# Windowed attention and a softplus feed-forward on one core: downs two slots later, GpSimd's attention work moved, weights converted between the first heads

## The chip, the cores and the metric

The kernel runs on one core of a Trainium2 chip. The metric is device time in microseconds (us). The engines are TensorE (PE, matmuls, with its weight loads shown apart as PEld), VectorE (DVE), ScalarE (ACT), GpSimd (POOL) and SyncE (SP, which here only issues DMAs).

## The reference

Inputs are q, k, v of 8 batches, 8 heads, 576 positions and 64 values per head, and two weights, 512 x 2048 and 2048 x 512, drawn at random; q, k and v are float32, the weights float64.

```python
scores = (q @ k.T) / sqrt(64)               # per batch and head
mask   = 0 <= i - j < 64                    # a causal window of 64 positions
attn   = softmax(where(mask, scores, -1e9)) # the sum gets + 1e-9
x      = (attn @ v) as 4608 tokens x 512
h      = x @ w_in                           # 4608 x 2048
g      = maximum(h, 0) + log1p(exp(-abs(h)))
out    = g @ w_out                          # 4608 x 512
```

## The kernel before

**Tiling.** Tokens are cut into 12 blocks g of 384 (`TB`), the 8 heads into 4 head pairs hp, the 2048 inner features into 16 chunks f of 128. For float32 precision nearly every matrix is split into a high and a low part (`x0/x1`, `g0/g1`, `w..0/w..1`), and a product is three matmuls: high-high, high-low, low-high.

**Feed-forward.** A step (g, f) is an *up* (`ffn_up`, 12 matmuls of L391 into one of two `ps_h` buffers; then abs, exp, ln on ACT in L395 to L397, the softplus sum L399 on DVE, which is the last reader of `ps_h`, the cast L401 to the high part and the subtraction L402 to the low part) and a *down* (`ffn_down`, 9 matmuls of L412 into the three accumulators `ps_o`). After the last chunk of a block L430 copies `ps_o` to a tile `raw`, and DMAs write it out. The order of steps is `passes`: block 0 with its first 8 chunks (its partial sums go to DRAM and are added again later, L428), block 1 with all 16, block 0 with the other 8, then blocks 2 to 11, 192 steps in all.

**Weights.** `load_w(f)` fetches chunk f as 64-bit words (1 MB, each float64 seen as two 32-bit words), makes float32 of them with one ACT and four DVE instructions (L165 to L169), and splits them: cast on ACT (L172), subtraction on POOL (L173). Even and odd chunks go through two sets of buffers (`raw`/`osb`, `raws`/`ws`).

**Attention.** `attention(g, hp)` is a generator in stages: loads, splitting of q and k (L238 to L243), scores of three sub-blocks (L258 with the masked minimum L265), softmax (L271 to L281) with the splitting of the probabilities (L300 to L308, a transpose by DMA) and of v (L316 to L320), and two stages of attn @ v, one per head (L367, L372, L373), the second of which splits the result to `x_t` by the helper `split` (L150, L151). Blocks 0 and 1 (`by_pe`) take another way: block-diagonal k tiles (`kbd`), transposes on PE (L288), padded v tiles (`v_pad`), in plain float32.

**The order of the work.** Every stage and step gets a place in slots, two slots per step: an up of step n at 2n + 0.5, its down at 2n + 3.5, weights of chunk f at 12 slots (`AHEAD`) before the step that first uses them, an attention stage at the base of its block and head pair plus an offset of its stage (`BASE`, `PACE`, `STG0`, `STG2` for blocks 0 to 2; 8 slots per head pair, `SHP`, for the others). The program is emitted in the order of these places. A planner then orders each engine's queue by priority and by its own costs; from slot 100 on (`PE_ORDERED_FROM`, step 50) PE's queue alone keeps the written order. Tiles of one name (or tag) share `bufs` buffers, and a new one waits until the old one's last reader is done.

Of the kernel before, what the change touches and what calls it, by code (L numbers as in the profile page):

```python
# [15 lines left out]
P = 128  # L16
# [5 lines left out]
NCH = TB // CH + 1  # L22

SPLIT = 8
AHEAD = 12
BASE = (-100, -46, 2 * (SPLIT + 16) - 24)
PACE = (5, 5, 5)
STG0 = (-6, -6, 1, 2, 3, 4, 7, 8)
STG2 = (-10, -5, 0, 1, 2, 3, 14, 15)
STG = (-14, -8, 0, 1, 2, 3, 15, 17)  # L30
SH, SHP = -13, 8
PE_ORDERED_FROM = 100
# [6 lines left out]
def window_attention_softplus_ffn(  # L39
# [70 lines left out]
    for t in range(2):  # L110
        nc.gpsimd.memset(kbd[D:P, t, 0, :], 0.0)
        nc.gpsimd.memset(kbd[0:D, t, 1, :], 0.0)
        nc.gpsimd.memset(kbd[0:D, t, 0, 0:CH], 0.0)
        nc.gpsimd.memset(kbd[D:P, t, 1, 0:CH], 0.0)

# [15 lines left out]
    ident = cpool.tile([P, P], F32, name="ident")  # L131
# [6 lines left out]
    pt_s = spare(1, [P, 2, 2, TB], F32, "pt")  # L138


    v_pads = []
    for n in range(NP):
        t = spare(2 + n, [P, 2, NJ, 2, P], F32, f"v_pad{n}")
        (nc.gpsimd if n else nc.vector).memset(t, 0.0)
        v_pads.append(t)

    mm, tp = nc.tensor.matmul, nc.tensor.transpose

    def split(dst_hi, dst_lo, src, e_hi, e_lo):
        e_hi.tensor_copy(dst_hi, src)  # L150
        e_lo.tensor_tensor(dst_lo, src, dst_hi.bitcast(F32), ALU.subtract)  # L151

    def load_w(f):


        if f % 2 and f < NE + 4:
            raw, w = spare(6, [P, 2, DM], w_words.dtype, "raws"), spare(7, [P, 2, DM], F32, "ws")
        else:
            raw = ff.tile([P, 2, DM], w_words.dtype, name="raw", bufs=1)
            w = ff.tile([P, 2, DM], F32, name="osb", bufs=1)  # L160
        nc.sync.dma_start(raw, w_words[f])
        words = raw.bitcast(U32).rearrange("p m (n two) -> p two m n", two=2)
        low, high = words[:, 0, :, :], words[:, 1, :, :]
        wb = w.bitcast(U32)
        nc.scalar.activation(w, high.bitcast(F32), AF.Abs)  # L165
        nc.vector.tensor_scalar(w, w, ZERO_HIGH, None, ALU.max)
        nc.vector.tensor_scalar(wb, wb, 3, 0x3FFFFFF8, ALU.logical_shift_left, ALU.bitwise_and)
        nc.vector.scalar_tensor_tensor(wb, high, 0xC0000000, wb, ALU.bitwise_and, ALU.bitwise_or)
        nc.vector.scalar_tensor_tensor(wb, low, 29, wb, ALU.logical_shift_right, ALU.bitwise_or)  # L169
        for m in range(2):  # L170
            hi, lo = [weight(m, i, f) for i in range(2)]
            nc.scalar.copy(hi, w[:, m, :])  # L172
# [6 lines left out]
    def attention(g, hp):  # L179
# [15 lines left out]
        if by_pe:  # L195
            qf = ld.tile([P, 2, TB], F32, name="q_in") if hp % 2 else ld.tile([P, 2, W - P + TB], F32, name="k_in")
            qf = qf[:, 0, 0:TB]
            kf = kbd[:, hp % 2, :, :]
# [4 lines left out]
            v_pad = v_pads[hp]  # L203

            def load_v(rows, lay, j0, start):
                n = rows.stop - rows.start
                for j in range(j0, NJ):
                    dst = v_pad[rows, lay, j, :, :].rearrange("p h (i d) -> p (h i) d", i=2)[:, 0:4:3, :]
                    s = start + j * P
                    nc.sync.dma_start(dst, v[s : s + n, c0 : c0 + P].rearrange("p (h d) -> p h d", h=2))  # L210

            if t0 == 0:
                dst = v_pad[CH:P, 0, 0, :, :].rearrange("p h (i d) -> p (h i) d", i=2)[:, 0:4:3, :]
                nc.sync.dma_start(dst, v[0:CH, c0 : c0 + P].rearrange("p (h d) -> p h d", h=2))
            load_v(slice(0, P), 0, 1 if t0 == 0 else 0, t0 - CH)
            load_v(slice(0, CH), 1, 0, t0 + CH)
            load_v(slice(CH, P), 1, 0, t0)
        else:
            q_in = ld.tile([P, 2, TB], F32, name="q_in")
            k_in = ld.tile([P, 2, W - P + TB], F32, name="k_in")  # L220
            v_in = ld.tile([P, NCH, P], F32, name="v_in")
            ts, ks = slice(t0, t0 + TB), slice(t0 - CH, t0 + TB)
            for half in heads:
                nc.sync.dma_start(
                    q_in[half, :, :], qT[c0 : c0 + P, ts].rearrange("(h d) t -> d h t", h=2)
                )
                nc.sync.dma_start(
                    k_in[half, :, :], kT[c0 : c0 + P, ks].rearrange("(h d) t -> d h t", h=2)
                )
            for half in heads:  # L230
                nc.sync.dma_start(v_in[half, :, :], v[ks, c0 : c0 + P].rearrange("(c p) n -> p c n", p=CH))
        yield

        if not by_pe:
# [8 lines left out]
            nc.vector.tensor_tensor(k_lo, k_in, k_hi.bitcast(F32), ALU.subtract)  # L243
# [37 lines left out]
        nc.vector.tensor_tensor(pn, pn, sm.unsqueeze(2).to_broadcast([P, 2 * NJ, P]), ALU.mult)  # L281
        if by_pe:

            pt = pt_s[:, hp % 2, :, :]
            for hh in range(2):
                pp = bank()
                for j in range(NJ):
# [2 lines left out]
        else:  # L290
# [15 lines left out]
            nc.gpsimd.tensor_tensor(part(1, 0), pv[0], part(0, 1), ALU.subtract)  # L306
# [9 lines left out]
            nc.scalar.copy(v12[:, :, :, 0, :], vv)  # L316
            nc.vector.tensor_tensor(vv, vv, v12[:, :, :, 0, :], ALU.subtract)  # L317
            nc.scalar.copy(v12[:, :, :, 1, :], vv)  # L318
            nc.gpsimd.tensor_tensor(v13[low, :, :, :], vv[low, :, :, :], v12[low, :, :, 1, :], ALU.subtract)  # L319
            nc.vector.tensor_copy(v13[up, :, :, :], v12[up, :, :, 0, :])  # L320
        yield

# [11 lines left out]
        for hh in range(2):  # L334
# [48 lines left out]
    def ffn_up(g, f):  # L383
# [13 lines left out]
        nc.scalar.activation(u, u, AF.Ln, bias=1.0)  # L397
        gf = u
        nc.vector.scalar_tensor_tensor(gf, hv, 0.0, u, ALU.max, ALU.add)  # L399
        gt = [ff.tile([P, TB], F32R, name=f"g{i}", bufs=2) for i in range(2)]  # L400
        (nc.scalar.copy if g == 0 else nc.vector.tensor_copy)(gt[0], gf)  # L401
        (nc.vector if g >= 2 else nc.gpsimd).tensor_tensor(gt[1], gf, gt[0].bitcast(F32), ALU.subtract)  # L402
        gs[g, f] = gt

    def ffn_down(g, f, first, last):
# [10 lines left out]
        if last:  # L416
            rows = out[ORDER[g] * TB : (ORDER[g] + 1) * TB, :]
            spill, fill = f < NF - 1, f == NF - 1 and g in part
            if spill:
                part[g] = rows = dram.tile([TB, DM], F32, name="part")  # L420
            o = ff.tile([P, 2, DM], w_words.dtype, name="raw", bufs=1).bitcast(F32).rearrange("p a n -> p (a n)").rearrange("p (j n) -> p j n", n=DM)
            for j0, j1 in ((0, 2), (2, 3)):
                rs = slice(j0 * P, j1 * P)
                if fill:
                    nc.sync.dma_start(o[:, j0:j1, :], part[g][rs, :].rearrange("(j p) n -> p j n", p=P))
                for j in range(j0, j1):
                    if fill:
# [82 lines left out]
```

## Time and profile before

| what | value |
|---|---|
| median of 3 runs | 1280.91 us (1280.70 to 1281.58) |
| the profiled execution | 1280.53 us, span 1278.7 us |
| granted TensorE clock, mean | 0.912 |
| PE busy | 1092.9 us (85%), 5888 matmuls |
| DVE busy | 849.5 us (66%) |
| ACT busy | 690.9 us (54%) |
| POOL busy | 295.5 us (23%) |

A line of the profile names engine, line of the kernel, operation, tiles written <- read, shapes, count, busy time and the mean of one in ns, then the idle time of the engine before these instructions and what ended it. "PE ps_o L412 <- DVE g L401" reads: PE's matmuls of line 412 stood idle until DVE's instruction of line 401 was done. In the chart of the span in 40 equal slices a digit is the share of a slice in tenths:

```profile
PE   6668888799999887888878887888878888889998
DVE  5389997376866677666775667666775666666433
POOL 2046455442311112111212112211212112212000
PEclk9668988889999899898988989899898998889999
```

Matmuls overlap, so the duration of one is longer than its share of the time; the distance from start to start tells what a group costs.

### The profile page before, as it was taken

The page shows a single profiled execution, that of the slowest core. Times are in us where ns is not written, and L with a number is a line of the kernel's source. Part 1 is how long each engine was busy: PE and PEld are TensorE (multiplying, and loading weights), DVE is VectorE, ACT ScalarE, POOL GpSimd, SP SyncE. Part 2 cuts the span into 40 slices and gives each one's busy share as a digit, 9 for nine tenths or more (in the row PEclk, how much of TensorE's full clock was granted, in tenths as well). Part 3 has the DMA queues.
Part 4 walks back from the last instruction along what each step waited for, and adds up shares of the span by engine and source line. Part 5 has one row for each costly group of instructions (what it writes and reads, how often), then busy time and mean ns, then how long its engine had stood idle before and what let it go on. Part 6 is the DMA issues. An engine that isn't in the chain of part 4 may idle for free.

```text
span 1278.7 us, 17049 instructions
## 1 busy us (share of the span) xinstructions
PE 1092.9 (85%) x5888; PEld 936.3 (73%) x5888; DVE 849.5 (66%) x1764; ACT 690.9 (54%) x1565; POOL 295.5 (23%) x208
## 2 busy tenths in 40 slices
PE   6668888799999887888878887888878888889998
PEld 4557667577788776777767776777767777678897
DVE  5389997376866677666775667666775666666433
ACT  3356765376755556555655556555554555555333
POOL 2046455442311112111212112211212112212000
PEclk9668988889999899898988989899898998889999
DMA  3464563175533245433442334422442344433000
GB/s 94 104 207 139 162 168 102 66 147 126 123 76 91 66 79 125 87 66 91 94 104 68 91 81 95 113 67 66 116 107 67 91 82 91 92 64 65 26 1 25
DMA packets 209175, 119.09 MB, mean 93 GB/s; under 512 B 143296, under 2 KB 201664, under 8 KB 207040
## 3 DMA queue, kind: packets, MB, share of 16 engines
q1 hardware_dynamic: 209088, 118.00, 38.5%
q8 instruction: 46, 0.75, 0.2%
q14 instruction: 41, 0.34, 0.1%
HBM read 76.28 MB, written 10.22 MB: 68 GB/s over the span
## 4 chain that ended last, share of the span: by engine, by line
PE 56%; DVE 30%; issue 6%; DMA 4%; ACT 2%; SPq 1%; DVEq 0%; ACTq 0%
PE ps_o L412 26%; PE ps_h L391 21%; PE ps_a L367 5%; DVE k L243 5%; PE ps_a L258 3%; DVE st L281 3%; DVE st L265 3%; DVE q_hl L240 3%; DVE v_in L317 2%; DVE u L399 2%; DVE st L271 2%; DVE xf L373 1%; DMA raw<-in_w_words_dram 1%; DVE g L401 1%; DMA tr<-nat 1%
## 5 line engine op out<-in xcount | busy, mean ns | idle before, releaser
L412 PE MATMUL ps_o<-w,g 128*128 128x512 f32 x1728 | 487.5, 428 | 121.3 <-DVE g L401 117.5
L412 PEld LDWEIGHTS ps_o<-w,g 128*128 128x128 f32 x1728 | 338.4, 204 | 209.9 <-DVE g L401 121.9
L391 PE MATMUL ps_h<-x,w 128*128 128x384 f32 x2304 | 474.2, 355 | 16.0 <-ACT w L172 10.4
L391 PEld LDWEIGHTS ps_h<-x,w 128*128 128x128 f32 x2304 | 432.8, 201 | 35.4 <-ACT w L172 11.5
L395 ACT ACTIVATE u<-ps_h 128x384 f32<-128x384 f32 x192 | 93.5, 487 | 279.6 <-PE ps_h L391 274.1
L399 DVE SCALAR_TENSOR_TENSOR u<-ps_h,u 128x384 f32<-128x384 f32 x192 | 106.1, 553 | 206.9 <-ACT u L397 206.6
L319 POOL TENSOR_TENSOR v<-v_in,v 64x896 bf16<-64x896 f32 x40 | 78.7, 1968 | 436.7 <-ACT v L318 418.7
L306 POOL TENSOR_TENSOR nat<-st,nat 128x768 bf16<-128x768 f32 x40 | 69.9, 1747 | 262.2 <-ACT nat L302 261.9
L275 ACT ACTIVATE st<-st,mn 128x128 f32<-128x128 f32 x288 | 111.7, 389 | 31.5 <-DVE st L271 31.4
L265 DVE CUSTOM_DVE_ANT_0 st<-ps_a,mask 128x192 f32<-128x192 f32 x216 | 68.4, 354 | 65.9 <-PE ps_a L258 52.5
L396 ACT ACTIVATE u<-u 128x384 f32<-128x384 f32 x192 | 100.4, 525 | 4.4
L397 ACT ACTIVATE u<-u 128x384 f32<-128x384 f32 x192 | 99.7, 521 | 4.4
L402 DVE TENSOR_TENSOR g<-u,g 128x384 fp32r<-128x384 f32 x160 | 91.1, 569 | 9.6 <-DVE g L401 0.5
L367 PEld LDWEIGHTS <-v 128*128 128x128 bf16 (+1 forms) x1088 | 61.9, 105 | 37.4 <-issue 17.7
L258 PE MATMUL ps_a<-k,q_hl 128*128 128x192 f32 x480 | 77.2, 288 | 10.9 <-DVE q_hl L240 6.2
L367 PE MATMUL ps_a<-tr,v 128*64 128x128 bf16 (+3 forms) x1088 | 80.7, 217 | 6.8 <-DMA tr<-nat 5.0
L258 PEld LDWEIGHTS ps_a<-k,q_hl 128*128 128x128 f32 x480 | 69.0, 199 | 14.6 <-DVE q_hl L240 7.0
L401 DVE CAST g<-u 128x384 fp32r<-128x384 f32 x176 | 69.6, 396 | 9.3 <-PE ps_o L412 1.8
L243 DVE TENSOR_TENSOR k<-k_in,k 128x896 fp32r<-128x896 f32 x40 | 68.3, 1707 | 1.9 <-ACT k L239 1.9
L302 ACT CAST nat<-st 128x768 bf16<-128x768 f32 x40 | 33.3, 831 | 54.7 <-DVE st L301 54.6
L150 DVE CAST x<-xf 128x384 fp32r<-128x384 f32 x40 | 56.8, 1419 | 7.9 <-PE ps_h L391 7.7
L372 ACT COPY xf<-ps_a 64x384 f32<-64x384 f32 x80 | 38.1, 476 | 41.2 <-PE ps_a L367 40.1
(83 smaller groups left out, 1010.0 us busy)
## 6 DMA issues: line engine op xcount, KB each, us to landing
v_in<-in_v_dram SPq DMA_DIRECT2D x80, 224.0 KB, 3.5
k_in<-in_kT_dram SPq DMA_DIRECT2D x80, 224.0 KB, 3.8
q_in<-in_qT_dram SPq DMA_DIRECT2D x84, 192.0 KB, 3.7
raw<-in_w_words_dram SPq DMA_DIRECT2D x10, 1024.0 KB, 4.9
raws<-in_w_words_dram SPq DMA_DIRECT2D x6, 1024.0 KB, 5.2
out_dram<-raw SPq DMA_DIRECT2D x12, 512.0 KB, 2.8
out_dram<-raw SPq DMA_DIRECT2D x12, 256.0 KB, 2.8
v_pad<-in_v_dram SPq DMA_DIRECT2D x52, 32.0 KB, 2.1
```

Of the source, the lines that this page charges most:

```text
L243: nc.vector.tensor_tensor(k_lo, k_in, k_hi.bitcast(F32), ALU.subtract)
L258: mm(spv[:, hh, :], q_hl[:, hh, js], part[:, hh, kc], start=(hh == 0 and i == 0), stop=(hh == 1 and i == 1), skip_group_check=True,)
L265: nc.vector.tensor_tensor_reduce(st[:, hh, j, :], spv[:, hh, :], m, QSCALE, 3.0e38, ALU.add, ALU.min, mn[:, hh, j : j + 1])
L275: nc.scalar.activation(sv[:, i, 0:P], sv[:, i, 0:P], AF.Exp, bias=mn[:, hh, j : j + 1], scale=-1.0, accum_out=sm[:, i : i + 1])
L367: mm(av[: D if s else P, osl], v13[:, c, hh, :] if s else v12[:, c, hh, :, :], src, start=(i == 0), stop=(i == len(passes) - 1), skip_grou ...
L391: mm(hv, weight(0, a, f)[:, c * P : (c + 1) * P], x[b][c], start=(i_mm == 0), stop=(i_mm == 3 * NC - 1))
L395: nc.scalar.activation(u, hv, AF.Abs)
L396: nc.scalar.activation(u, u, AF.Exp, scale=-1.0)
L397: nc.scalar.activation(u, u, AF.Ln, bias=1.0)
L399: nc.vector.scalar_tensor_tensor(gf, hv, 0.0, u, ALU.max, ALU.add)
L402: (nc.vector if g >= 2 else nc.gpsimd).tensor_tensor(gt[1], gf, gt[0].bitcast(F32), ALU.subtract)
L412: mm(ops[g][j], gt[a][:, js], weight(1, b, f), start=(first and i == 0), stop=(last and i == 2),)
```

## The change

- A down is placed at 2n + 5.5 instead of 2n + 3.5 (`DOWN`), and the `g` tiles get three buffers each instead of two.
- Attention work of POOL goes to DVE: L306 (low part of the probabilities) and L319 (low part of v). The helper `split` goes: the cast to `x_t[0]` runs on ACT instead of DVE (L150), the subtraction to `x_t[1]` on DVE instead of POOL (L151). In `ffn_up` the subtraction L402 is always on DVE (POOL did it for blocks 0 and 1), and the cast L401 is on ACT for blocks 0 and 1 and for odd chunks of the others (before: for block 0 alone).
- The weights get written-out places (`CONVERT`): chunks 0 to 3 at slots -104 to -88, between the heads of block 0, the others from slot -6 to 24. They use four pairs of spare buffers for chunks 0 to 7, two pairs for 8 to 11, and halves in the tiles `v_in` and `v12` of the attention for 12 to 15.
- `BASE`, `PACE`, `STG0`, `STG2` get new values. Block 1's first pair moves from slot -46 to -10, block 2's from 24 to 29.
- Buffers: `kbd` becomes two tiles, `v_pad` two tiles instead of four, `pt`, `ident` share tags with attention tiles; `raw` is half as large with two buffers. DMA loads of v are issued in the second stage, after those of q and k.

The diff, cut to its core:

```diff
-AHEAD = 12
-BASE = (-100, -46, 2 * (SPLIT + 16) - 24)
-PACE = (5, 5, 5)
-STG0 = (-6, -6, 1, 2, 3, 4, 7, 8)
-STG2 = (-10, -5, 0, 1, 2, 3, 14, 15)
+DOWN = 5.5
+CONVERT = (-104, -98, -93, -88, -6, -3, 0, 3, 6, 8, 11, 13, 16, 18, 21, 24)
+BASE = (-100, -10, 29)
+PACE = (5, 4, 4.5)
+STG0 = (-4.5, 0.5, 1, 2, 3, 4, 7, 8)
+STG2 = (-6, -3, 0, 1, 2, 3, 12, 13)
 STG = (-14, -8, 0, 1, 2, 3, 15, 17)
...
-    kbd = spare(0, [P, 2, 2, W - P + TB], F32, "kbd")
+    kbd_s = [att.tile([P, 2, CH + TB], F32, name="kbd", tag=f"k{i}") for i in range(2)]
...
+    v_pads = [att.tile([P, 2, NJ, 2, P], F32, name="v_pad", tag=n) for n in ("nat", "tr")]
+    for t in v_pads:
+        nc.vector.memset(t, 0.0)
...
-    for n in range(NP):
-        t = spare(2 + n, [P, 2, NJ, 2, P], F32, f"v_pad{n}")
-        (nc.gpsimd if n else nc.vector).memset(t, 0.0)
-        v_pads.append(t)
...
-        if f % 2 and f < NE + 4:
-            raw, w = spare(6, [P, 2, DM], w_words.dtype, "raws"), spare(7, [P, 2, DM], F32, "ws")
+        if f < NE + 4:
+            k = (0, 4, 2, 6)[f % 4] if f < NE else (4, 6)[f % 2]
+            parts = [(spare(k, [P, 2, DM], w_words.dtype, "raws"), spare(k + 1, [P, 2, DM], F32, "ws"), 0, 2)]
         else:
-            raw = ff.tile([P, 2, DM], w_words.dtype, name="raw", bufs=1)
-            w = ff.tile([P, 2, DM], F32, name="osb", bufs=1)
+            parts = [
+                (
+                    ff.tile([P, 1, DM], w_words.dtype, name="raw"),
+                    att.tile([P, 1, DM], F32, name="wh", tag=("v_in", "v12")[m]),
+                    m, m + 1,
+                )
+                for m in range(2)
+            ]
...
-            nc.gpsimd.tensor_tensor(part(1, 0), pv[0], part(0, 1), ALU.subtract)
+            nc.vector.tensor_tensor(part(1, 0), pv[0], part(0, 1), ALU.subtract)
...
-            nc.gpsimd.tensor_tensor(v13[low, :, :, :], vv[low, :, :, :], v12[low, :, :, 1, :], ALU.subtract)
+            nc.vector.tensor_tensor(v13[low, :, :, :], vv[low, :, :, :], v12[low, :, :, 1, :], ALU.subtract)
...
-                split(x_t[0], x_t[1], xf, nc.vector, nc.gpsimd)
+                nc.scalar.copy(x_t[0], xf)
+                nc.vector.tensor_tensor(x_t[1], xf, x_t[0].bitcast(F32), ALU.subtract)
...
-        gt = [ff.tile([P, TB], F32R, name=f"g{i}", bufs=2) for i in range(2)]
-        (nc.scalar.copy if g == 0 else nc.vector.tensor_copy)(gt[0], gf)
-        (nc.vector if g >= 2 else nc.gpsimd).tensor_tensor(gt[1], gf, gt[0].bitcast(F32), ALU.subtract)
+        gt = [ff.tile([P, TB], F32R, name=f"g{i}", bufs=3) for i in range(2)]
+        (nc.scalar.copy if g < 2 or f % 2 else nc.vector.tensor_copy)(gt[0], gf)
+        nc.vector.tensor_tensor(gt[1], gf, gt[0].bitcast(F32), ALU.subtract)
...
-            events.append((2 * n - AHEAD, lambda f=f: load_w(f)))
+            events.append((CONVERT[f], lambda f=f: load_w(f)))
...
-        events.append((2 * n + 3.5, lambda step=steps[n]: ffn_down(*step)))
+        events.append((2 * n + DOWN, lambda step=steps[n]: ffn_down(*step)))
```

More of the change, by code (lines that the diff above doesn't have):

```diff
@@ L108, in window_attention_softplus_ffn @@
     W = CH + P
-    kbd = spare(0, [P, 2, 2, W - P + TB], F32, "kbd")
[L110 to L114, printed above, removed]
+    kbd_s = [att.tile([P, 2, CH + TB], F32, name="kbd", tag=f"k{i}") for i in range(2)]
+    for t in kbd_s:
+        nc.gpsimd.memset(t[D:P, 0, :], 0.0)
+        nc.gpsimd.memset(t[0:D, 1, :], 0.0)
+        nc.gpsimd.memset(t[0:D, 0, 0:CH], 0.0)
+        nc.gpsimd.memset(t[D:P, 1, 0:CH], 0.0)
+    v_pads = [att.tile([P, 2, NJ, 2, P], F32, name="v_pad", tag=n) for n in ("nat", "tr")]
+    for t in v_pads:
+        nc.vector.memset(t, 0.0)
     FAR = BIG / QSCALE
@@ L130, in window_attention_softplus_ffn @@
     nc.gpsimd.memset(mask_c[:, 0:CH], FAR)
-    ident = cpool.tile([P, P], F32, name="ident")
+    ident = att.tile([P, P], F32, name="ident", tag="xf")
     make_identity(nc, ident)
@@ new lines, in load_w @@
+        for raw, w, m0, m1 in parts:
+            nc.sync.dma_start(raw, w_words[f][:, m0:m1, :])
+            words = raw.bitcast(U32).rearrange("p m (n two) -> p two m n", two=2)
+            low, high = words[:, 0, :, :], words[:, 1, :, :]
+            wb = w.bitcast(U32)
+            nc.scalar.activation(w, high.bitcast(F32), AF.Abs)
+            nc.vector.tensor_scalar(w, w, ZERO_HIGH, None, ALU.max)
+            nc.vector.tensor_scalar(wb, wb, 3, 0x3FFFFFF8, ALU.logical_shift_left, ALU.bitwise_and)
+            nc.vector.scalar_tensor_tensor(wb, high, 0xC0000000, wb, ALU.bitwise_and, ALU.bitwise_or)
+            nc.vector.scalar_tensor_tensor(wb, low, 29, wb, ALU.logical_shift_right, ALU.bitwise_or)
+            for m in range(m0, m1):
+                hi, lo = [weight(m, i, f) for i in range(2)]
+                nc.scalar.copy(hi, w[:, m - m0, :])
+                nc.gpsimd.tensor_tensor(lo, w[:, m - m0, :], hi.bitcast(F32), ALU.subtract)
@@ L197, in attention @@
             qf = qf[:, 0, 0:TB]
-            kf = kbd[:, hp % 2, :, :]
+            kf = kbd_s[hp % 2]
             skip = CH if t0 == 0 else 0
@@ L202, in attention @@
                 nc.sync.dma_start(kf[heads[hh], hh, skip:], kT[c0 + hh * D : c0 + (hh + 1) * D, t0 - CH + skip : t0 + TB])
-            v_pad = v_pads[hp]
+        else:
+            q_in = ld.tile([P, 2, TB], F32, name="q_in")
+            k_in = ld.tile([P, 2, W - P + TB], F32, name="k_in")
+            ts, ks = slice(t0, t0 + TB), slice(t0 - CH, t0 + TB)
+            for half in heads:
+                nc.sync.dma_start(
+                    q_in[half, :, :], qT[c0 : c0 + P, ts].rearrange("(h d) t -> d h t", h=2)
+                )
+                nc.sync.dma_start(
+                    k_in[half, :, :], kT[c0 : c0 + P, ks].rearrange("(h d) t -> d h t", h=2)
+                )
+        yield
+        if by_pe:
+            v_pad = v_pads[hp % 2]
             def load_v(rows, lay, j0, start):
@@ L218, in attention @@
         else:
[L219 to L229, printed above, removed]
+            v_in = att.tile([P, NCH, P], F32, name="v_in")
             for half in heads:
                 nc.sync.dma_start(v_in[half, :, :], v[ks, c0 : c0 + P].rearrange("(c p) n -> p c n", p=CH))
-        yield
-        if not by_pe:
             q_hl = att.tile([P, 2, TB], F32R, name="q_hl")
@@ L282, in attention @@
         if by_pe:
-            pt = pt_s[:, hp % 2, :, :]
+            pt = att.tile([P, 2, TB], F32, name="pt", tag="q_hl")
             for hh in range(2):
@@ L420, in ffn_down @@
                 part[g] = rows = dram.tile([TB, DM], F32, name="part")
-            o = ff.tile([P, 2, DM], w_words.dtype, name="raw", bufs=1).bitcast(F32).rearrange("p a n -> p (a n)").rearrange("p (j n) -> p j n", n=DM)
             for j0, j1 in ((0, 2), (2, 3)):
+                o = ff.tile([P, 1, DM], w_words.dtype, name="raw").bitcast(F32)
+                o = o.rearrange("p m (j n) -> p (m j) n", n=DM)[:, : j1 - j0, :]
                 rs = slice(j0 * P, j1 * P)
                 if fill:
-                    nc.sync.dma_start(o[:, j0:j1, :], part[g][rs, :].rearrange("(j p) n -> p j n", p=P))
+                    nc.sync.dma_start(o, part[g][rs, :].rearrange("(j p) n -> p j n", p=P))
                 for j in range(j0, j1):
                     if fill:
-                        nc.vector.tensor_tensor(o[:, j, :], o[:, j, :], ops[g][j], ALU.add)
+                        nc.vector.tensor_tensor(o[:, j - j0, :], o[:, j - j0, :], ops[g][j], ALU.add)
                     else:
-                        (nc.scalar.copy if j == 1 else nc.vector.tensor_copy)(o[:, j, :], ops[g][j])
-                nc.sync.dma_start(rows[rs, :].rearrange("(j p) n -> p j n", p=P), o[:, j0:j1, :])
+                        (nc.scalar.copy if j == 1 else nc.vector.tensor_copy)(o[:, j - j0, :], ops[g][j])
+                nc.sync.dma_start(rows[rs, :].rearrange("(j p) n -> p j n", p=P), o)
     passes = [(0, 0, SPLIT), (1, 0, NF), (0, SPLIT, NF)] + [(g, 0, NF) for g in range(2, NB)]
```

18 lines of the change are left out of this document (removed).

## The prediction

> **What bounds the kernel now.** I read the span, then busy times by stretch of the span, then how many up steps fall into each stretch (one L395 each), then one period of the steady part instruction by instruction.
>
> ```profile
> span 1278.7 us, 17049 instructions
> 0.00:50.00 50.00, 34.69 (x169) 24.71 (x170) 24.28 (x94) 17.33 (x70) 8.66 (x24) 0.94 0.40 100
> 50.00:78.00 28.00, 12.76 (x55) 9.55 (x54) 13.62 (x38) 10.55 (x33) 0.00 (x0) 0.62 0.61 174
> 78.00:210.00 132.00, 107.79 (x526) 93.17 (x527) 126.12 (x181) 83.79 (x183) 75.35 (x47) 0.83 0.54 154
> 210.00:305.00 95.00, 82.37 (x432) 70.88 (x431) 53.64 (x100) 53.14 (x111) 40.59 (x32) 0.93 0.39 95
> 402.00:1146.00 744.00, 634.50 (x3484) 544.03 (x3484) 500.86 (x1068) 410.63 (x925) 138.47 (x85) 0.91 0.38 88
> 1146.00:1206.00 60.00, 59.53 (x358) 52.22 (x357) 31.75 (x67) 29.00 (x60) 8.73 (x6) 1.00 0.20 35
> ...
> 78.00:210.00 132.00, 8.22 (x17) 0.83 0.54 154
> 210.00:305.00 95.00, 7.32 (x16) 0.93 0.39 95
> 402.00:1146.00 744.00, 55.00 (x114) 0.91 0.38 88
> ```
>
> The first rows give stretch, length, then busy time (and count) of PE, weight load, DVE, ACT and POOL, then granted clock, DMA share and GB/s; the last three give ACT busy in L395 alone. Three regimes are to be seen. Up to 305 us there are 17 + 16 = 33 ups; DVE is full from 78 to 210 us (126.12 of 132), and no up runs before 78 us. From 402 to 1146 us 114 ups take 744 us, 6.53 us each, so 26.1 us for the four steps that go with one head pair ("a period"; 114/4 = 28.5 of them). There PE is busy 85% at clock 0.91, and DVE 67%: no engine is full. From 1146 to 1206 us PE is full at clock 1.00. So the steady part loses time to a wait, and this is the one:
>
> ```profile
> PE ps_o L412 <- DVE g L401: 107.1, 29, 4.1
> PE ps_h L391 <- ACT w L172: 10.4, 2, 10.0
> ...
> 597.98 2.25 PE L412 MATMUL ps_o<-w,g 128*128 128x512 f32 x9
> 609.11 0.58 PE L258 MATMUL ps_a<-k,q_hl 128*128 128x192 f32 x4
> 609.53 2.26 PE L412 MATMUL ps_o<-w,g 128*128 128x512 f32 x9
> 611.63 2.27 PE L391 MATMUL ps_h<-x,w 128*128 128x384 f32 x12
> 617.67 3.79 PE L412 MATMUL ps_o<-w,g 128*128 128x512 f32 x9 [3.77 <-DVE g L401]
> 621.29 2.27 PE L391 MATMUL ps_h<-x,w 128*128 128x384 f32 x12
> 623.40 2.25 PE L412 MATMUL ps_o<-w,g 128*128 128x512 f32 x9
> ```
>
> The first row, from the waits of 402 to 1146 us, says 29 waits of a down for the cast L401, 3.7 us each: one per period. A period without it: from the down at 597.98 to the up at 611.63 lie 13.65 us, which hold three downs, two ups, both value groups and all three score groups; two ups at 2.11 (621.29 to 623.40) and one down at 2.10 (609.53 to 611.63) complete it: 20.0 us. The other 6.1 us are the 3.77 us wait and 2.3 us of slow clock behind it (the down at 617.67 takes 3.6 us to the next start instead of 2.1).
>
> Why the g of the up just before the score group of 609.11 is late is seen on ACT and DVE:
>
> ```profile
> 609.83 0.49 ACT L395 ACTIVATE u<-ps_h 128x384 f32<-128x384 f32 x1
> 614.89 0.51 ACT L397 ACTIVATE u<-u 128x384 f32<-128x384 f32 x1
> ...
> 610.30 1.76 DVE L150 CAST x<-xf 128x384 fp32r<-128x384 f32 x1
> 612.45 1.90 DVE L243 TENSOR_TENSOR k<-k_in,k 128x896 fp32r<-128x896 f32 x1
> 615.79 0.96 DVE L281 TENSOR_TENSOR st<-st,sm 128x768 f32<-128x768 f32 x1
> 616.67 0.55 DVE L399 SCALAR_TENSOR_TENSOR u<-ps_h,u 128x384 f32<-128x384 f32 x1
> 617.25 0.36 DVE L401 CAST g<-u 128x384 fp32r<-128x384 f32 x1
> ```
>
> Between its first and last activation ACT runs the next pair's casts and six exponentials, and DVE runs L243 to L281. The up ended near 609.3; L399, which frees its ps_h, ends at 617.22, and L401 at 617.61.
>
> **Downs two slots later, three g buffers.** Behind an up PE now does the down before it, the next up and then the down of this g; it becomes down, up, down, up, and then the down of this g. That down has some 6.5 us of work more ahead of it, so L401 and L402 stop being waited for; the third g pair pays for the longer life. Late next is ps_h, which has two buffers: the up two steps on needs L399, not L401. Behind the score group that up could start at 609.53 + 2.10 + 2.11 + 2.10 = 615.84. L399 ends at 617.22 in today's order of ACT and DVE: a wait of 1.4 us instead of 3.77. The x cast that goes to ACT may fall into that chain (+0.5). Floor 0, if ACT and DVE get another order; ceiling 3.5, if every moved vector instruction also lands ahead of L399 (below). I take 1.6, nearest to today's rows.
>
> Does a wait of 1.6 us still cost clock? Nearest rows, from the start:
>
> ```profile
> 186.48 2.33 PE L412 MATMUL ps_o<-w,g 128*128 128x512 f32 x9 [0.92 <-DVE g L401]
> 193.82 0.59 PE L367 MATMUL ps_a<-tr,v 128*128 128x64 bf16 x7 [1.80 <-DMA tr<-nat]
> ...
> 187.30:190.60 3.30, 2.94 (x13) 1.91 (x11) 3.30 (x5) 3.30 (x14) 1.87 (x2) 1.00 0.81 181
> 194.10:197.50 3.40, 1.11 (x12) 0.83 (x9) 3.33 (x4) 1.21 (x2) 0.61 (x1) 0.50 0.89 201
> ```
>
> Idle time of 0.92 us left the next 3.4 us at 1.00, 1.80 us was followed by 0.50. A wait of 1.6 us is nearer to the second, but falls whole into one such stretch only about half the time ((3.4 - 1.6)/3.4); then 3.4 us at half speed cost 1.7. I take 0.9 as the mean, floor 0, ceiling today's 2.3. A new period is 20.0 + 1.6 + 0.9 = 22.5 us, 3.6 less than now: 28.5 x 3.6 = 103 us. The Trainium skill, TensorE: Matmul & The Clock Gate, section HAM oscillation, sets the bound at PE gaps over about 3.4 us; by that rule the 1.6 us would cost no clock and the sum would be the 1100 of the second rival, while the 1.80 us row speaks against it.
>
> **GpSimd's attention work.** Prices:
>
> ```profile
> L319 POOL TENSOR_TENSOR v<-v_in,v 64x896 bf16<-64x896 f32 x40 | 78.7, 1968 | 436.7 <-ACT v L318 418.7 <-PE ps_a L367 7.7 <-issue 6.0
> L306 POOL TENSOR_TENSOR nat<-st,nat 128x768 bf16<-128x768 f32 x40 | 69.9, 1747 | 262.2 <-ACT nat L302 261.9
> L301 DVE TENSOR_TENSOR st<-st,nat 128x768 f32<-128x768 f32 x40 | 38.9, 971 | 0.3 <-ACT nat L300 0.2
> L317 DVE TENSOR_TENSOR v_in<-v_in,v 128x896 f32<-128x896 f32 x40 | 44.8, 1119 | 5.5 <-ACT v L316 5.5
> L402 DVE TENSOR_TENSOR g<-u,g 128x384 fp32r<-128x384 f32 x160 | 91.1, 569 | 9.6 <-DVE g L401 0.5
> L150 DVE CAST x<-xf 128x384 fp32r<-128x384 f32 x40 | 56.8, 1419 | 7.9 <-PE ps_h L391 7.7
> L401 DVE CAST g<-u 128x384 fp32r<-128x384 f32 x176 | 69.6, 396 | 9.3 <-PE ps_o L412 1.8
> ```
>
> Per period DVE gains L306 at L301's 0.97, L319 at L317's 1.12 and the x subtraction at L402's 0.57; it loses L150's 1.42 and two of four casts L401 at 0.40: 2.66 - 2.22 = +0.4 on 500.86/28.5 = 17.6, so 18.0 of 22.5 us. ACT gains three casts at L397's 0.51: 410.63/28.5 = 14.4 becomes 15.9. Both stay under PE, so the mean cost is nothing, and PE's work hides it. What is not hidden is the order: L306 waits for ACT's L302 and L319 for L318, on POOL a harmless wait (436.7 and 262.2 us idle); on DVE the next L399 queues behind it, and the up on PE behind that. L150 at 1.76 us beside a POOL instruction, against 0.36 for the same shape as L401, is what goes in exchange. Both are bounded by the 0 and 3.5 above.
>
> **Start: weights between the first heads, BASE, PACE, STG0, STG2.**
>
> ```profile
> 50.00:305.00 255.00, 45.04 (x40) 22.73 (x30) 31.67 (x20) 0.84 0.49 134
> 50.00:305.00 255.00, 32.18 (x24) 13.78 (x18) 19.84 (x12) 0.84 0.49 134
> 3.18 5.01 SPq L210 DMA_DIRECT2D v_pad<-in_v_dram  x8
> ```
>
> The first two rows are DVE, ACT and POOL time on the tiles osb and ws: sixteen conversions cost DVE 77.2 us, 4.8 each. Today none is done before the end of the first heads, and the first up waits 10.0 us for L172. Four moved into the first 50 us raise DVE there from 24.3 to 43.5 us: it fits. POOL and ACT have 41 and 33 us free. On SP the four weight loads join queues of which the v_pad loads are the longest piece (5.01 us per eight); these now follow the q and k loads, which start the scores, so I cost SP at nothing, floor -2, ceiling +5. The first up then comes near 50 us. What DVE still owes up to the 33rd up: 24.3 + 13.6 + 126.1 + 53.6 = 217.6, less 43.5, is 174; plus 32 g subtractions from POOL at 0.57 (18) and four pairs' L306 and L319 with half of L150 gone (5) is 197; at the 126.12/132 = 0.955 of today's full stretch 206 us. So the 33rd up comes at 256 us by DVE, while PE would need about 235 (33 ups and downs of 4.2; g=1's four head pairs at 7, since 34.69 us in the first 50 held about five; g=2's at the 3.2 that 20.0 leaves beside four steps; 185 us behind the first 50). Less POOL work beside DVE speeds its copies, so I take 253, 52 us earlier than 305; ends 20 and 70 us. The later order of g=1 (BASE -10) is paid out of this: its attention lies inside the 206 us, where before it lay ahead of the first up.
>
> **At nothing, together.** Two kbd and two v_pad tiles instead of larger ones, ident in the tag of xf, the half-size raw tiles with two buffers and v_in's later load each wait for a tile that was last read some slots before; the memsets shrink on POOL. Cover gone, each is a DMA of some microseconds, once per pair at worst. Weights 12 to 15 in halves add about twenty small DVE instructions, 3 us, inside the 206. The stretches 305 to 402 (97), 1146 to 1206 (60) and from 1206 us on (72.7) stay: PE is already nearly full there.
>
> **Sum.** 1278.7 - 103 - 52 = 1123.7 us span; 1.8 us lie around the span in the profiled execution (1280.53), which is 0.4 under the median 1280.91. Forecast 1125 us, 12% less.
>
> **Rivals.**
> 1. No wait is left: ACT and DVE get an order in which L397 and L399 go ahead of the exponentials and L281. For it: ACT needs 15.9 and DVE 18.0 of 20.0 us. Against: today's order repeats in all 29 periods. Period 20.0, 28.5 x 6.1 = 174 saved: 1055 us.
> 2. The wait shrinks to 1.6 us and the clock stays full, as behind the 0.92 us row: 28.5 x 4.5 = 128 saved: 1100 us. Against: the 1.80 us row.
> 3. The wait moves whole from L412 to L391: x cast (0.5), L319 (1.1) and their waits for ACT come ahead of L399 and make the wait 3.5 us with 2.2 us of slow clock; period 25.7, 11 saved: 1217 us. For it: ps_h keeps two buffers, and L399 today is only 0.4 us ahead of L401.
> 4. Slower: DVE's queue stands behind ACT at both L306 and L319 while the next pair's L240 and L243 queue too, so that the scores come late as well. It decides from the point where a period loses 6.1 + 52/28.5 = 7.9 us, that is L399 some 4 us later than today; at 9 us a period (9 - 7.9) x 28.5 = 31 over: 1312 us. Against: DVE's total is 18.0. The same page of the Trainium skill (TensorE: Matmul & The Clock Gate, Architectural detail) calls ACT and DVE strictly first in, first out, which is the condition for this; every row above is in keeping.
>
> **Numbers.** Forecast 42% (own range 1090 to 1165), rival 1 20%, rival 2 13%, rival 3 17%, slower 6%, within 0.2% 2% (0.2% is about what a measurement of this kernel can tell from no change). The range 1055 to 1205 leaves out half of the first rival's and of the third's spread and the rest. Faster 0.92, same 0.02, slower 0.06.
>
> **What would show it.** Right: the waits list loses L412 <- L401 and shows L391 <- DVE u L399 with 1 to 2 us, once per period; the granted clock from 400 us rises over 0.93; the first up starts near 50 us and POOL is idle after the weights. Wrong: L391 <- L399 over 3 us (rival 3), or none (rival 1); DVE over 95% busy or PE waiting for scores (rival 4); DVE short of full before 250 us with no earlier 33rd up (start).

## The result, and the profile after

The changed kernel takes 1093.17 us against 1280.81, a ratio of 0.8536 (95% interval 0.8517 to 0.8555). The profiled execution took 1091.76 us with a span of 1090.0. Most line numbers shift by four to six. In the feed-forward part L391 is now L396, L395 L400, L397 L402, L399 L404, L401 L406, L402 L407 and L412 L417; in the attention L243 is now L247, L271 L275, L275 L279, L278 L282 and L281 L285, and the cast to `x_t[0]`, L150 before, is L379.

From the page, the span, the busy times and the chart of the granted clock:

```profile
span 1090.0 us, 16756 instructions
PE 1011.9 (93%) x5888; PEld 882.7 (81%) x5888; DVE 826.5 (76%) x1797; ACT 743.1 (68%) x1705; POOL 53.4 (5%) x53
PEclk8889789999999999999999999999999999999999
```

From the seventh slice on the clock is full. PE's busy time for the same 5888 matmuls fell by 81 us (1092.9 to 1011.9), and most of that is the clock: 189 us of PE's busy time lay in stretches at half clock before, 39 us do now, so 75 us less are lost there. Then the stretches (columns as before: length, PE, weight load, DVE, ACT, POOL, clock, DMA share, GB/s) and, in the last three rows, ACT in L400 alone, whose count is the number of ups:

```profile
58.00:160.00 102.00, 78.03 (x375) 68.63 (x375) 95.32 (x179) 64.72 (x149) 37.99 (x24) 0.83 0.48 156
160.00:262.00 102.00, 99.71 (x590) 85.85 (x590) 76.60 (x168) 79.00 (x184) 0.00 (x0) 1.00 0.54 119
262.00:354.00 92.00, 90.22 (x558) 79.71 (x557) 75.66 (x169) 67.79 (x153) 0.00 (x0) 1.00 0.56 116
354.00:960.00 606.00, 576.76 (x3494) 505.59 (x3493) 482.11 (x1067) 441.44 (x1011) 0.00 (x0) 1.00 0.45 108
...
50.00:58.00 8.00, 0.47 (x1) 1.00 0.92 322
58.00:160.00 102.00, 5.23 (x11) 0.83 0.48 156
160.00:262.00 102.00, 9.88 (x21) 1.00 0.54 119
```

1 + 11 + 21 = 33 ups now lie before 262 us instead of 305. Behind 354 us the same steps as those of 402 to 1146 us take some 138 us less: from the first matmul of the 52nd up to that of the 165th it is 738.6 us before and 600.2 now, so 26.1 and 21.2 us per period. What is left of the wait there, and one period on PE (`...` marks lines left out):

```profile
PE ps_h L396 <- DVE u L404: 29.1, 28, 1.1
...
659.09 2.35 PE L396 MATMUL ps_h<-x,w 128*128 128x384 f32 x12 [1.05 <-DVE u L404]
...
672.50 0.59 PE L262 MATMUL ps_a<-k,q_hl 128*128 128x192 f32 x4
672.93 2.23 PE L417 MATMUL ps_o<-w,g 128*128 128x512 f32 x9
674.99 2.27 PE L396 MATMUL ps_h<-x,w 128*128 128x384 f32 x12
677.10 2.25 PE L417 MATMUL ps_o<-w,g 128*128 128x512 f32 x9
680.39 1.86 PE L396 MATMUL ps_h<-x,w 128*128 128x384 f32 x9 [1.05 <-DVE u L404]
```

The down no longer waits. Once per period an up waits 1.05 us for L404, the last reader of its ps_h. The main lines of the chain behind it on ACT and DVE:

```profile
673.25 0.49 ACT L400 ACTIVATE u<-ps_h 128x384 f32<-128x384 f32 x1
675.20 0.51 ACT L379 CAST x<-xf 128x384 fp32r<-128x384 f32 x1
676.03 0.39 ACT L279 ACTIVATE st<-st,mn 128x128 f32<-128x128 f32 x1
678.35 0.51 ACT L402 ACTIVATE u<-u 128x384 f32<-128x384 f32 x1
...
674.95 0.56 DVE L275 TENSOR_TENSOR st<-st 128x384 f32<-128x384 f32 x1
675.42 1.08 DVE L247 TENSOR_TENSOR k<-k_in,k 128x896 fp32r<-128x896 f32 x1
678.48 0.17 DVE L282 TENSOR_SCALAR sm<-sm 128x6 f32<-128x6 f32 x1 [0.39 <-ACT st L279]
678.91 0.96 DVE L285 TENSOR_TENSOR st<-st,sm 128x768 f32<-128x768 f32 x1
679.79 0.55 DVE L404 SCALAR_TENSOR_TENSOR u<-ps_h,u 128x384 f32<-128x384 f32 x1
```

The six exponentials (L279) still run ahead of L402, and L285 ahead of L404. The x cast (L379) has indeed joined ACT's chain.

### The profile page after: what moved, and what is told of

The parts are those of the page before. It is cut to its first block, busy times and chain, and to the rows that moved or that the text cites. A ratio compares the mean times of both kernels' runs of the same rounds, so it can differ in the third digit from the quotient of the medians.

```text
span 1090.0 us, 16756 instructions
## 1 busy us (share of the span) xinstructions
PE 1011.9 (93%) x5888; PEld 882.7 (81%) x5888; DVE 826.5 (76%) x1797; ACT 743.1 (68%) x1705; POOL 53.4 (5%) x53
## 4 chain that ended last, share of the span: by engine, by line
PE 58%; ACT 17%; DVE 16%; DMA 4%; issue 3%; SPq 1%; ACTq 0%
PE ps_h L396 25%; PE ps_o L417 23%; ACT st L279 6%; PE ps_a L371 6%; PE ps_a L262 4%; DVE st L285 3%; DVE v_in L321 3%; ACT k L243 2%; ACT q_hl L242 2%; DVE st L269 2%; DVE u L404 2%; ACT u L400 1%; ACT v L322 1%; ACT u L401 1%; ACT x L379 1%
## 5 line engine op out<-in xcount | busy, mean ns | idle before, releaser
L396 PE MATMUL ps_h<-x,w 128*128 128x384 f32 x2304 | 454.2, 345 | 41.6 <-DVE u L404 40.9
L396 PEld LDWEIGHTS ps_h<-x,w 128*128 128x128 f32 x2304 | 404.6, 190 | 69.2 <-DVE u L404 56.5
L417 PE MATMUL ps_o<-w,g 128*128 128x512 f32 x1728 | 433.3, 394 | 0.7 <-DVE g L407 0.7
L417 PEld LDWEIGHTS ps_o<-w,g 128*128 128x128 f32 x1728 | 316.7, 188 | 57.7 <-DVE g L407 1.1
L400 ACT ACTIVATE u<-ps_h 128x384 f32<-128x384 f32 x192 | 93.5, 487 | 143.0 <-PE ps_h L396 126.6
L404 DVE SCALAR_TENSOR_TENSOR u<-ps_h,u 128x384 f32<-128x384 f32 x192 | 106.1, 553 | 77.0 <-ACT u L402 76.0
L407 DVE TENSOR_TENSOR g<-u,g 128x384 fp32r<-128x384 f32 x192 | 105.6, 550 | 24.2 <-ACT g L406 22.6
L279 ACT ACTIVATE st<-st,mn 128x128 f32<-128x128 f32 x288 | 111.5, 391 | 14.1 <-DVE st L275 14.1
L402 ACT ACTIVATE u<-u 128x384 f32<-128x384 f32 x192 | 100.2, 522 | 4.4
L401 ACT ACTIVATE u<-u 128x384 f32<-128x384 f32 x192 | 100.7, 525 | 3.4
L406 ACT CAST g<-u 128x384 fp32r<-128x384 f32 x112 | 57.3, 511 | 40.5 <-DVE u L404 40.2
L371 PE MATMUL ps_a<-tr,v 128*64 128x128 bf16 (+2 forms) x1088 | 78.3, 215 | 0.0
L322 ACT CAST v<-v_in 128x896 bf16<-128x896 f32 x40 | 37.5, 938 | 40.5 <-DVE v_in L321 40.5
L310 DVE TENSOR_TENSOR nat<-st,nat 128x768 bf16<-128x768 f32 x40 | 38.3, 957 | 23.7 <-ACT nat L306 23.7
L279 ACT ACTIVATION_READ_ACCUMULATOR st<-st,mn 128x1 f32 x288 | 54.5, 189 | 0.0
L285 DVE TENSOR_TENSOR st<-st,sm 128x768 f32<-128x768 f32 x48 | 50.2, 1047 | 1.3
L377 DVE TENSOR_TENSOR xf<-ps_a,xf 64x384 f32<-64x384 f32 x80 | 44.0, 550 | 5.8 <-ACT xf L376 3.6
```

Source lines behind the costliest of these rows:

```text
L279: nc.scalar.activation(sv[:, i, 0:P], sv[:, i, 0:P], AF.Exp, bias=mn[:, hh, j : j + 1], scale=-1.0, accum_out=sm[:, i : i + 1])
L371: mm(av[: D if s else P, osl], v13[:, c, hh, :] if s else v12[:, c, hh, :, :], src, start=(i == 0), stop=(i == len(passes) - 1), skip_grou ...
L396: mm(hv, weight(0, a, f)[:, c * P : (c + 1) * P], x[b][c], start=(i_mm == 0), stop=(i_mm == 3 * NC - 1))
L400: nc.scalar.activation(u, hv, AF.Abs)
L401: nc.scalar.activation(u, u, AF.Exp, scale=-1.0)
L407: nc.vector.tensor_tensor(gt[1], gf, gt[0].bitcast(F32), ALU.subtract)
```

## The experiments

**Does the later down carry the steady part?** Theory A says yes and that the wait then is one for ps_h; theory B says that GpSimd's move does it. `down_only` is the kernel before with one line changed:

```diff
-        events.append((2 * n + 3.5, lambda step=steps[n]: ffn_down(*step)))
+        events.append((2 * n + 5.5, lambda step=steps[n]: ffn_down(*step)))
```

> The kernel before with its downs at 2n + 5.5 and nothing else (two g buffers stay). Theory A, the later down carries the steady part: the wait L412 <- L401 of 3.7 us goes, an up waits for L399 instead, 1.4 us once a period, and a second pair of g buffers is enough, since a down follows its next-but-one up at once; period 21.4 to 22.3 us instead of 26.1, start unchanged: 1145 to 1175 us. Theory B, GpSimd's move carries it: the wait only changes its place, over 3 us long, and the time stays over 1230 us.

Measured 1140.18 us, ratio 0.8903 (0.8885 to 0.8922). Its waits of PE, from 400 to 1000 us, and its busy times from 354 to 950 us:

```profile
PE ps_h L391 <- DVE u L399: 35.7, 27, 1.3
...
354.00:950.00 596.00, 562.65 (x3392) 492.14 (x3392) 480.95 (x1040) 392.86 (x895) 130.71 (x82) 1.00 0.46 107
```

The wait is where and as long as the prediction worked out from the old order of ACT and DVE (1.38 us, measured 1.3), the clock is full, and two g buffers are enough here. This one line alone brings 141 of the 188 us. The time lies 5 us under theory A's range: the period is 21.6 us, as A said, but the part before the 52nd up, which A left unchanged, became 10 us shorter too. `down_back` is the changed kernel with `DOWN = 3.5`.

> The changed kernel with its downs back at 2n + 3.5. Theory A: the down waits again for L406, about 3.6 us once a period (L406 ends at 680.73 in the changed kernel's period, the down would be due at 677.10), with about 2 us of slow clock behind it; period 25.9 us instead of 21.3, 28.5 of them: about 1225 us. Theory B: under 1130 us.

Measured 1222.85 us, ratio 0.9549 (0.9529 to 0.9569): 130 us lost again. The wait and one instance of it:

```profile
PE ps_o L417 <- DVE g L406: 94.9, 27, 3.5
624.52 3.85 PE L417 MATMUL ps_o<-w,g 128*128 128x512 f32 x9 [3.50 <-DVE g L406]
```

A was right to within 2 us here and missed by 5 us above; B falls.

**What is GpSimd's attention work worth?** `pool_back` puts it back into the changed kernel:

```diff
-            nc.vector.tensor_tensor(part(1, 0), pv[0], part(0, 1), ALU.subtract)
+            nc.gpsimd.tensor_tensor(part(1, 0), pv[0], part(0, 1), ALU.subtract)
...
-                nc.scalar.copy(x_t[0], xf)
-                nc.vector.tensor_tensor(x_t[1], xf, x_t[0].bitcast(F32), ALU.subtract)
+                nc.vector.tensor_copy(x_t[0], xf)
+                nc.gpsimd.tensor_tensor(x_t[1], xf, x_t[0].bitcast(F32), ALU.subtract)
```

(and the subtraction of v13 likewise).

> The changed kernel with the attention's three instructions as before: low parts of the probabilities and of v on GpSimd, x cast on DVE and x subtraction on GpSimd. Theory A: the cast of x takes 1.7 us beside GpSimd again, ACT's chain loses the x cast (0.4), so the wait L396 <- L404 is between 0.8 and 1.4 us: 1085 to 1105 us. Theory B: DVE runs late again, the wait grows over 2 us and takes slow clock with it: 1140 us or more.

Measured 1099.7 us, ratio 0.8591 (0.8576 to 0.8607), 6 us over the changed kernel. Its waits from 354 to 960 us, and the group of the k split in it and, below, in the changed kernel:

```profile
PE ps_h L396 <- DVE u L404: 37.6, 28, 1.4
...
L247 DVE TENSOR_TENSOR k<-k_in,k 128x896 fp32r<-128x896 f32 x40 | 69.4, 1735 | 0.0
```

```profile
L247 DVE TENSOR_TENSOR k<-k_in,k 128x896 fp32r<-128x896 f32 x40 | 43.9, 1098 | 0.0
```

The wait is 0.3 us longer, which is 28.5 x 0.3 = 8.5 us; the 52nd up comes 2 us earlier, and so 6 us are all that the move brings. Its way is also to be seen: without GpSimd beside it the same split takes 1.10 us instead of 1.74. The Trainium skill (SBUF — State Buffer, section Who interferes with whom) says that a vector instruction with two SBUF inputs contends with a GpSimd instruction that reads SBUF, and calls what they share an exclusive lock. The trace of `pool_back` agrees: the split at 440.90 us, 0.25 us behind the start of a GpSimd subtraction (L380), took 1.90 us and ended 0.95 us after that one did, while the split at 162.37 us, with a GpSimd subtraction that began 0.51 us after it, took 1.08 us.

**Is the wait left one for a ps_h buffer?** `psh3` takes a PSUM buffer from ps_a for ps_h:

```diff
-    ps_a = ctx.enter_context(tc.tile_pool(name="ps_a", bufs=3, space=bass.MemoryType.PSUM))
-    ps_h = ctx.enter_context(tc.tile_pool(name="ps_h", bufs=2, space=bass.MemoryType.PSUM))
+    ps_a = ctx.enter_context(tc.tile_pool(name="ps_a", bufs=2, space=bass.MemoryType.PSUM))
+    ps_h = ctx.enter_context(tc.tile_pool(name="ps_h", bufs=3, space=bass.MemoryType.PSUM))
```

> The changed kernel with three ps_h buffers and two ps_a buffers instead of two and three. Theory A, the wait L396 <- L404 is one for a ps_h buffer: it goes, 35 waits of 1.05 us and some longer ones of the start, 40 us in all: 1050 to 1062 us. Rival: two ps_a buffers hold the scores and values back, PE waits at L262 or L371 for DVE's L269 or ACT's L376 instead: 1090 us or more.

Measured 1053.43 us, ratio 0.8232 (0.8216 to 0.8248), which beats both kernels, by 40 us the changed one. From 354 to 950 us PE waits for nothing:

```profile
354.00:950.00 596.00, 596.00 (x3661) 528.03 (x3660) 497.37 (x1108) 459.02 (x1048) 0.00 (x0) 1.00 0.50 113
```

A period takes 20.0 us there (52nd up to 165th: 564.7 us), the 20.0 that the prediction added up from the rows of before.

**What does a wait cost in clock?** The prediction took 0.9 us per period for a slow clock that did not come. In `abs1`, `abs2` and `abs4` the step whose L404 is waited for gets 1, 2 or 4 passes of the absolute value more, which change no value (the edit of `abs2`; by its two lines L402 becomes L404, L404 L406, L406 L408):

```diff
         nc.scalar.activation(u, hv, AF.Abs)
+        for _ in range(2 if g >= 2 and f % 4 == 2 else 0):
+            nc.scalar.activation(u, u, AF.Abs)
```

> The changed kernel with one more pass of the absolute value over u (no change of values) in every fourth step from block 2 on, the one whose L404 is waited for: the wait grows by one ACT pass, 0.45 us, to 1.5 us. Theory C, idle time of about 1.8 us within a stretch of 3.4 us already halves the next stretch's clock: at 1.5 us no slow clock or a few stretches, 1105 to 1112 us, clock 0.97. Theory D, only a gap of about 3.4 us does: none, 1106 us.

> The same with two more passes: the wait grows to about 2.0 us. Theory C: the wait falls whole into one stretch of 3.4 us in some 40% of the periods, each costing 1.7 us: 28.5 x (0.9 + 0.7) = 46 more than the changed kernel, about 1138 us, clock about 0.94. Theory D: no slow clock, 28.5 x 0.9 = 26 more: 1119 us, clock 0.97.

> The same with four more passes: the wait grows to about 2.9 us. Theory C: nearly every period has a slow stretch: 28.5 x (1.8 + 1.7) = 100 more, about 1193 us, clock about 0.91. Theory D: still none, 28.5 x 1.8 = 51 more: 1145 us, clock 0.97.

Measured 1097.26 us (ratio 0.8569, 0.8546 to 0.8592), 1144.0 (0.8934, 0.8916 to 0.8952) and 1210.03 (0.945, 0.9429 to 0.947). The waits in the steady part, in this order (L406 is here the softplus sum, L404 in the changed kernel):

```profile
PE ps_h L396 <- DVE u L406: 28.1, 27, 1.0
```

```profile
PE ps_h L396 <- DVE u L406: 47.7, 27, 1.8
```

```profile
PE ps_h L396 <- DVE u L406: 100.5, 28, 3.6
```

`abs1` missed its point: the wait stayed at 1.05 us, because the softplus sum stands behind L285 on DVE and not behind ACT: in the changed kernel L402 ends at 678.86 and L404 begins at 679.79, so a pass fits in between. Its time cannot be told from the changed kernel's. In `abs2` a 1.77 us wait has slow clock behind it in 18 of 28 periods, 64% where C said 40%; so theory D falls, and C's 1138 us is near the 1144. In `abs4` the wait is 3.6 us and not 2.9, since the order of the queues changed as well (L304 and L305 now run ahead of the softplus sum: in one period L305 begins at 499.72, behind a wait of 1.36 us for L304, and the sum at 500.87), and it has slow clock behind it in only 14 of 28 periods, which C did not expect. The clock changes only on a fixed grid of 3.41 us, and how PE's idle time lies in these stretches accounts for most of it. Two such stretches of `abs2`, and three of `abs4`:

```profile
663.26:666.67 3.41, 1.63 (x9) 1.20 (x8) 2.71 (x6) 2.77 (x7) 0.00 (x0) 1.00 0.90 224
666.67:670.09 3.42, 3.42 (x12) 3.14 (x11) 2.61 (x6) 2.53 (x5) 0.00 (x0) 0.50 0.00 0
```

```profile
472.36:475.77 3.41, 1.60 (x7) 0.95 (x6) 1.67 (x4) 3.41 (x11) 0.00 (x0) 1.00 0.98 257
475.77:479.18 3.41, 1.59 (x9) 1.59 (x10) 3.34 (x6) 2.53 (x6) 0.00 (x0) 1.00 0.22 54
479.18:482.60 3.42, 3.42 (x27) 2.76 (x26) 1.92 (x5) 1.54 (x3) 0.00 (x0) 1.00 0.00 0
```

1.78 us idle in one stretch halved the next one; a wait of 3.62 us cut in two by the limit, 1.81 and 1.82, halved none. Take all stretches of the kernel before, `down_back`, `abs2` and `abs4` behind 280 us that ran at full clock: none with less than 1.74 us idle was followed by a slow one, and each with more than 1.91 was. Between the two both are found, as in the rows above, so there the idle time alone does not decide. A stretch that itself runs slow is followed by another slow one far sooner. Of 118 such stretches 91, with at most 0.53 us idle, went back to full clock; 26 with 0.65 us or more and one with 0.33 did not. Two neighbours from the kernel before, the first with 0.9 us idle:

```profile
590.10:593.40 3.30, 2.41 (x6) 1.69 (x7) 3.16 (x8) 1.51 (x3) 0.00 (x0) 0.50 0.72 192
593.50:596.80 3.30, 3.30 (x11) 2.91 (x10) 0.44 (x1) 0.11 (x1) 1.77 (x1) 0.50 0.00 0
```

Without slow clock a period of `abs4` is 23.9 us, seven stretches of 3.413: the wait then keeps meeting the same limit, which is why it goes on for many periods.

**Which part of the change brings the start?** Four edits of the changed kernel, each undoing one part: weights 0 to 3 behind the first heads (`first4`), block 1's attention ahead of the first ups (`base_back`), two buffer pairs for the conversions (`spare_two`), the g subtraction of blocks 0 and 1 on GpSimd (`gsub_pool`); and `late8` with weights 8 to 15 at slots 20 to 24.

```diff
-CONVERT = (-104, -98, -93, -88, -6, -3, 0, 3, 6, 8, 11, 13, 16, 18, 21, 24)
+CONVERT = (-12, -10, -8, -7, -6, -3, 0, 3, 6, 8, 11, 13, 16, 18, 21, 24)           # first4
+CONVERT = (-104, -98, -93, -88, -6, -3, 0, 3, 20, 20.5, 21, 21.5, 22, 22.5, 23, 24) # late8
-BASE = (-100, -10, 29)
+BASE = (-100, -46, 29)                                                            # base_back
-            k = (0, 4, 2, 6)[f % 4] if f < NE else (4, 6)[f % 2]
+            k = (4, 6)[f % 2]                                                     # spare_two
-        nc.vector.tensor_tensor(gt[1], gf, gt[0].bitcast(F32), ALU.subtract)
+        (nc.vector if g >= 2 else nc.gpsimd).tensor_tensor(gt[1], gf, gt[0].bitcast(F32), ALU.subtract)  # gsub_pool
```

> The changed kernel with weights 0 to 3 converted at slots -12 to -7, behind the heads of block 0, instead of between them. Theory A, as predicted: 19 us of DVE work move out of the first 50 us into the stretch where DVE is full, so the 33rd up comes 15 to 20 us later: about 1110 us. Rival: the stretch from 58 to 160 us has room (PE waits there for other things, DVE 95 of 102 us): at most 5 us, under 1099 us.

> The changed kernel with the first value of BASE for block 1 back at -46, so that its attention lies ahead of the first ups again. Theory S1, DVE's total sets the start: the same work in another order, 1088 to 1099 us. Rival S2, moving block 1's attention behind the first ups is a gain of its own: PE waits for its first up again and the 33rd up comes 10 us later or more, 1103 us or more.

> The changed kernel with two pairs of buffers for the conversion of weights 0 to 11 instead of four for 0 to 7. Theory S1: DVE waits for nothing that more buffers would bring, 1090 to 1097 us. Rival S3, the four pairs are a part of the gain: a pair is held from the load to GpSimd's subtraction, some 10 us or more, so weights come late and the 33rd up with them, by 5 to 15 us: 1098 to 1108 us.

> The changed kernel with the subtraction L407 of blocks 0 and 1 on GpSimd again. Theory S1: 32 instructions of 0.57 us leave a full DVE, 18 us of its work, and the 33rd up comes 10 to 18 us earlier: 1075 to 1083 us. Rival S4: GpSimd takes 1.2 us for each beside its weights and holds DVE up, as the casts of 1.4 us instead of 0.36 show, and g comes later: within 4 us of the changed kernel, or slower.

> The changed kernel with weights 8 to 15 converted at slots 20 to 24, where before they were due at 20 to 34, instead of 6 to 24. Theory S5, what is left of the start's gain comes from these weights being done early, so that DVE's conversions no longer run beside block 0's second half: block 1's ups wait for them, and the 33rd up comes 10 to 25 us later, 1103 to 1118 us. Rival S6, the ups of block 1 come late enough anyway: under 1098 us.

| run | us | ratio to before (interval) | to the changed kernel |
|---|---|---|---|
| first4 | 1105.02 | 0.863 (0.8617 to 0.8642) | 12 slower |
| base_back | 1091.93 | 0.8524 (0.85 to 0.8549) | same |
| spare_two | 1092.61 | 0.8531 (0.851 to 0.8552) | same |
| gsub_pool | 1086.04 | 0.8479 (0.8459 to 0.8498) | 7 faster |
| late8 | 1085.58 | 0.8477 (0.8458 to 0.8496) | 8 faster |

Only undoing the four weights between the first heads costs time; the 33rd up (its L400) comes 13.5 us later, 275.4 instead of 261.9. The expected 1110 us and its rival's 1099 both missed the 1105, the first by less. In `first4` DVE's load is 29.8 us in the first 50 us and 105.7 of the 110 behind them; the third row is the changed kernel:

```profile
0.00:50.00 50.00, 34.17 (x154) 24.45 (x155) 29.77 (x96) 20.04 (x73) 6.08 (x22) 0.83 0.50 146
50.00:160.00 110.00, 85.64 (x401) 72.77 (x400) 105.70 (x167) 69.11 (x155) 46.29 (x30) 0.83 0.52 173
...
0.00:50.00 50.00, 34.47 (x144) 24.78 (x144) 38.16 (x101) 22.59 (x68) 15.46 (x29) 0.83 0.59 170
```

The new order of block 1 and the buffers bring nothing by themselves, and two edits made the kernel faster than the change did. Weights 8 to 15 need not be so early: in `late8` the 33rd up comes at 254.5 instead of 261.9, a gain that neither of its expectations had. The g subtractions are better on GpSimd, but `gsub_pool` lies between its two expectations, and why it gains stays open. In its trace DVE is no less busy up to 262 us (213.4 us, 213.6 in the changed kernel), since other instructions took longer (L275 813 ns instead of 624), and the 33rd up does not come earlier there (263.8). Its busy times up to 262 us:

```profile
sum 262.00, PE 226.01 PEld 190.71 DVE 213.42 ACT 172.20 POOL 91.55; mean PE 56.50 PEld 47.68 DVE 53.36 ACT 43.05 POOL 22.89
```

Of the 43 us by which the 33rd up comes earlier than before, the four weights are 12 to 14 and the later down 4 to 9: that up comes at 300.7 in `down_only` instead of 305.0, and at 270.4 in `down_back`. What makes up the rest stays open: not tried were the new stage offsets of blocks 0 to 2, the order of the v loads, the casts of block 1 on ACT, and taking several of these parts back at once.

## Why the prediction was right, and where its sizes were off

- *The wait moves from the down to the up, from L401 to L399 (now L404), once per period.* Right in place, number and cause: the waits lists of the changed kernel and of `down_only` show it, and `psh3` removes it by the buffer alone.
- *1.6 us of wait.* Measured 1.05. The term that was off is "the x cast may fall into that chain (+0.5)": it did, at 675.20, but two delays that went away were left out of this sum. Before, DVE's cast of x beside GpSimd (1.76 us) held L271 (now L275) back, for which ACT stood idle, and L243 (now L247) at 1.90 us held L278 (now L282) back. Counted from the start of the score group, the exponentials begin after 3.53 us now and 3.45 before, L282 after 5.98 us where L278 came after 6.25, and L404 ends after 7.84 us where L399 ended after 8.11. That is 0.27 us less than the 1.38 of the sum's first part, so 1.11. `pool_back`, with neither that relief nor the x cast on ACT, has a wait of 1.34, next to the 1.38.
- *0.9 us of slow clock per period.* Measured none from 160 us on. This was the larger miss. The prediction rightly took the 1.80 us row for a warning, but it weighed the length of that one wait; the stretch around it had shorter gaps too, 2.04 us idle in all:

```profile
190.70:194.00 3.30, 1.26 (x8) 0.76 (x8) 3.23 (x4) 3.28 (x8) 3.22 (x3) 1.00 0.64 121
```

  The limit for one stretch lies near 1.8 us, so a wait of 1.05 or 1.34 costs no clock, and the 1.6 forecast would have cost none either. Together the two terms are 28.5 x (22.5 - 21.2) = 37 us too much. The start was 9 us too little, and the stretch from the 33rd up to the 52nd, taken as unchanged, fell from 103.7 to 97.6 us between the L395 (now L400) of these ups: 37 - 9 + 6 = 34 against the 32 us by which the forecast was too long.
- *DVE stays under PE; the moved attention work costs nothing.* Right: DVE is 482.11 of 606 us in the steady part, POOL 0.
- *The start, 52 us.* Measured 43 (305 to 262). The first up begins at 23.8 us already and not near 50, though its L400 comes at 57.3. DVE is full as forecast (95.32 of 102 us from 58 to 160), but it does not set the end of the stretch: from 160 to 262 us PE is the full engine (99.71 of 102). (The 185 us that the prediction gave PE are also too many for their parts: 33 x 4.2, 4 x 7 and, with the four head pairs of block 2, 4 x 3.2 make 179.) That the g subtractions weigh on this start was right in sign (18 us of work, 7 us in time, in a way that the trace does not show); that block 1's new place costs nothing was right too.
- *The rivals.* The second, with a chance of 13%, came out in its mechanism, full clock, and its 1100 us was nearer to the 1093 than the forecast's 1125. So the time fell into the stated range, but of the forecast's two terms for a period only the wait came true, and not the slow clock behind it. The third, the whole wait moving on, and the fourth are refuted by the 1.05 us. The first said that another order of ACT and DVE would remove the wait; it took a third ps_h buffer instead, and then 1053 us, where it gave 1055.

## What to carry to other kernels

When a matmul waits for a result, count how much work the order lets the engine do first, and look at once for the next thing the longer pipeline holds: here a later down alone took a wait of 3.7 us to 1.3, and one more PSUM buffer for the ups took what the whole change had left of it (1.05). Price a stall together with the clock behind it, and shorten it below the point where clock is lost before chasing its last part. Undo the parts of a large change one by one: one line alone brought three quarters of this gain, and two parts were better left out or placed later.

## What the runs showed of the hardware

At full clock, what costs clock is not the length of a gap but PE's idle time inside a fixed stretch of 3.41 us: less than 1.74 us never slowed the next stretch, more than 1.91 always did, so that a wait of 1.77 us can cost more than one of 3.62 us cut in two. Inside a slow stretch 0.65 us of idle time was enough for a second one. The Trainium skill (TensorE: Matmul & The Clock Gate, Part 1) has this stretch of 3413 ns and says that it runs freely; the records agree, in that all changes of a run lie on one grid of 3.413 us. Its section HAM oscillation puts the bound at gaps of over about 3.4 us, where the measurement decides against it: waits of 1.77 us cost clock here.
